# Large tiles at multiples of 128 bytes in each partition, in a kernel of attention beside a Fourier transform

## The chip, the cores and the metric

The kernel runs on one core of a Trainium2 chip. The metric is the time of one execution on the device, in microseconds, as a median of several runs. The engines of the core are called PE (TensorE; PEld is its loading of weights), DVE (VectorE), ACT (ScalarE), POOL (GpSimd) and SP (SyncE, which issues the DMAs here). SBUF is the memory on the chip, 128 partitions, in each of which a tile takes a run of bytes; "place" below is a tile's first byte in the partition.

## What is computed

Two independent results stand beside each other in the output: attention with 32 heads that share one key and one value head, and the real part of a two-dimensional Fourier transform by matrices.

```python
# A: x [1,2048,1024], wq [1024,1024], wk, wv [1024,32], wo [1024,1024]
q = (x @ wq) as 32 heads of 32;  k = x @ wk;  v = x @ wv
p = softmax(q k^T * 32**-0.5);   a = concat_heads(p v) @ wo
# B: x [1,2048,1024], dft_seq [2048,2048] and dft_hid [1024,1024], real and imaginary
y = dft_seq_re @ (x @ dft_hid_re^T) - dft_seq_im @ (x @ dft_hid_im^T)
return concatenate([a, y], axis=-1)        # float32
```

## The kernel before

All work is recorded into one fixed order by a planner (class `Plan`) that knows a time for each task and keeps a queue for each of ACT, DVE, POOL and SP; PE's order is chosen along with it (the loop over `n` at the end of `tile_kernel`). On the chip each engine works through its list in that order.

*Products.* The large products (queries, both transforms, the output projection) go by a scheme of seven products for eight blocks (`PRODUCTS`). Each operand is split into a high and a low part, and three matmuls of 128 x 128 x 512 make one product: low and high of the left, `ml` and `mh`, as weights, and low and high of the right, `rl` and `rh`, as the moving operand, summed in a PSUM bank `psb` (`product`). The raw loads come into `m` and `r`; results leave over `h` and `y`. In the first products the parts of x and of the small weights lie in the tiles `p`.

*Attention* runs in 32 units (a block of 512 queries by four heads), each with 32 row steps and 32 column steps. A row step (`row`) multiplies the moving `kst` (the keys) by weights from `qst` (the queries) into `pss`; DVE takes its largest value into `nm`, and ACT the exponentials, whose sums go to `ls`. A column step (`col`) multiplies the moving `qst` by weights from `kst` into `pst`, and ACT writes its exponentials into `p`. A burst (`pv`) multiplies several `p` by `v`. Between these, PE fills in the products. Towards the end the last projections take their weights partly from `p` and from `rb`.

*The turned tile.* At the end of a unit's row steps (`open_unit`, from `t1` on) the row maxima and sums become the constants that the queries need. `md`, 32 numbers in each partition, holds two exponentials while this is worked out (a subtraction on POOL, an Exp on ACT, a product on POOL, a sum on DVE). The result, `m2`, is turned by PE and copied by DVE into `mt` (48 x 128, function `mt`), and three DMAs take it from there: two into `qst`, one to DRAM (`U.rows` and `rd`, kept in `U.sent`).

*Places.* Tiles of the pools of the left side are laid one after the other from the low end, those of the right side from the high end downwards. `m2` has 3 x 16 x 4 = 192 bytes, so what follows it starts 64 bytes past a multiple of 128. The high end itself is 96 bytes past one, and all right tiles have 2048 bytes. As built:

| tiles | first byte, before | past a multiple of 128, before | the same, after |
|---|---|---|---|
| ident, kst, v, m2 | 16512, 17024, 25216, 27264 | 0 | 0 |
| p (6 x 8192 bytes), qst (3 x 8192) | 27456, 76608 | 64 | 0 |
| nm, ls, md, mt | 101184 to 101824 | 64 | 0 |
| h, y, rb, ov | 102368 to 120800 | 96 | 0 |
| mh, ml, rh, rl | 122848 to 206816 | 96 | 0 |
| raw m and r | 208864 to 227296 | 96 | 0 |

The parts of a tile that a matmul takes lie multiples of 512 bytes behind its start (in `p` and `qst`, of 2048 or 512), so an operand has its tile's remainder. The two wkv tiles of the first products alone have parts of 256 bytes.

Of the kernel before, what the change touches and what calls it, by code (L numbers as in the profile page):

```python
# [9 lines left out]
F32 = mybir.dt.float32  # L10
F32R = mybir.dt.float32r
AF = mybir.ActivationFunctionType
ALU = mybir.AluOpType
AX = mybir.AxisListType
# [3 lines left out]
P = 128  # L18
# [7 lines left out]
NC = 16  # L26
# [164 lines left out]
def tile_kernel(ctx: ExitStack, tc, xT, wq, wkv, wo, xbT, wT, cT, out):  # L191
    nc = tc.nc
    te = Ordered(tc, nc.tensor)
    act = Ordered(tc, nc.scalar)
    dve = Ordered(tc, nc.vector)
    gp = Ordered(tc, nc.gpsimd)
# [3 lines left out]
    plan = Plan()  # L200

    def pool(name, bufs, **kw):
        kw.setdefault("reuse_waits", "tile")
        return ctx.enter_context(tc.tile_pool(name=name, bufs=bufs, **kw))
# [16 lines left out]
    keep = pool("keep", 1)  # L221
# [3 lines left out]
    dve.memset(kst[96:P, :].bitcast(F32), 0.0)  # L225
    dve.memset(kst[96:98, :].bitcast(F32), 1.0)
    v = keep.tile([P, NC, DH], F32, name="v")
    m2 = keep.tile([P, 3, NC], F32, name="m2")

    ps_s = pool("ps_s", 2, space=PSUM)  # L230
    ps_t = pool("ps_t", 1, space=PSUM)
# [2 lines left out]
    NY, NHR, NP, NQS = 5, 3, 6, 3  # L234
    NRR, NRM = 17, 4
    NT = {"r": (3, 2), "m": (3, 2)}
    stage = {k: pool(f"stage_{k}", 1, side="right") for k in "rm"}
    ringp = {k: pool(f"ring_{k}", 1, side="right") for k in "rm"}
    shape = {"r": [P, W], "m": [P, 4, P]}
    raw = {k: [Ring(stage[k], f"{k}{a}", NT[k][a], shape[k], F32) for a in range(2)] for k in "rm"}  # L240
    ringn = {"r": NRR, "m": NRM}
# [11 lines left out]
    sm = pool("sm", 2)  # L253
# [368 lines left out]
    NU, SU, LEAD, PACE = len(units), 32, 12, 4  # L622
# [7 lines left out]
    def place_of(u, r):  # L630

        return (r % 16, r // 16) if u == 0 else divmod(r, 2)
# [115 lines left out]

    nmr = Ring(sm, "nm", 2, [P, 2, NC], F32)
    lsr = Ring(sm, "ls", 2, [P, 2, NC], F32)  # L750
    mdr = Ring(sm, "md", 1, [P, 2, NC], F32)
    rowT, colT = [Task() for _ in range(total)], [Task() for _ in range(total)]
    rexp, cexp = [Task() for _ in range(total)], [Task() for _ in range(total)]
    pvT = [[Task() for _ in bursts[u]] for u in range(NU)]
    pvC = [[Task() for _ in range(NC)] for _ in range(NU)]
    unit = []
# [6 lines left out]
    def open_unit(u):  # L763
        b, g = units[u]
        U = Unit()
# [4 lines left out]
        for r, (a, d) in enumerate((("qh", qh_d), ("ql", ql_d), ("qh", qh_d))):  # L770
            U.open.append(plan.task("sp", ISSUE, lambda r=r, d=d: move(
                U.q.tile[r * DH:(r + 1) * DH], d[b][g].rearrange("(h d) c -> d h c", d=DH)),
                deps=[landed[a, b, g]], order=U.open[:1], prio=at, kb=256))
        U.q.users += [rowT[u * SU + SU - 1], colT[u * SU + SU - 1]]
        U.nm, U.ls, U.md = nmr.take(), lsr.take(), mdr.take()
        mx = None
        for r in range(SU):
            s = u * SU + r
            i, j = place_of(u, r)

            def top(r=r, s=s, i=i, j=j):
# [3 lines left out]
            mx = plan.task("dve", 1.22, top, deps=[rowT[s], *(U.nm.deps if r == 0 else ())], prio=first_p + s - 44)  # L785
            plan.task("act", 1.22, lambda s=s, i=i, j=j: act.activation(
                rowps[s], rowps[s], AF.Exp, bias=U.nm.tile[:, j, i:i + 1], accum_out=U.ls.tile[:, j, i:i + 1]),
                deps=[mx], prio=first_p + s - 43.6, into=rexp[s],
                order=[cexp[s - SU - LEAD - EXTRA]] if s >= SU + LEAD + EXTRA else [])

        T = {}

        def dv(us, f, *deps):
            return plan.task("dve", us, f, deps=deps, prio=-1e4)

        def gv(us, f, *deps):
            return plan.task("pool", us, f, deps=deps, prio=-1e4, port=True)

        def least(to):
            dve.tensor_reduce(to, U.nm.tile.rearrange("p j i -> p i j"), axis=AX.X, op=ALU.min)  # L800

        def t1():
            mdr.make(U.md)
            least(m2[:, 2])
        prev = [unit[u - 1].turn.done] if u else []
        a = dv(0.2, t1, mx, *U.md.deps, *prev)
        c = dv(0.2, lambda: least(m2[:, 0].bitcast(F32R)), mx, *prev)
        a = gv(0.3, lambda: gp.tensor_sub(U.md.tile, m2[:, 2].unsqueeze(1).to_broadcast([P, 2, NC]), U.nm.tile), a)
        e = plan.task("act", 0.24, lambda: act.activation(U.md.tile, U.md.tile, AF.Exp), deps=[a], prio=-1e4)
        c = gv(0.3, lambda: gp.tensor_sub(m2[:, 1], m2[:, 2], m2[:, 0]), c, a)  # L810
        a = gv(0.3, lambda: gp.tensor_mul(U.md.tile, U.md.tile, U.ls.tile), e, rexp[u * SU + SU - 1], rexp[u * SU + SU - 2])
        a = dv(0.2, lambda: dve.tensor_reduce(m2[:, 2], U.md.tile.rearrange("p j i -> p i j"), axis=AX.X, op=ALU.add), a, c)
        U.nm.users.append(a)
        U.ls.users.append(a)
        U.md.users.append(a)
        a = dv(0.25, lambda: dve.reciprocal(m2[:, 2], m2[:, 2]), a)
        U.turn = Odd(lambda bank: te.transpose(bank[:3 * NC, :P], m2.rearrange("p a b -> p (a b)"), ident), [a, c], 0.2, -1)

        def mt():
            T["mt"] = sm.tile([3 * NC, P], F32, name="mt", bufs=1)  # L820
            dve.tensor_copy(T["mt"], U.turn.bank[:3 * NC, :P])
        a = U.turn.freed = dv(0.27, mt, U.turn.done, *(unit[u - 1].sent if u else []))
        odds.append(U.turn)
        U.rows = [plan.task("sp", ISSUE, lambda k=k: move(
            U.q.tile[96 + k:97 + k].rearrange("o h (t c) -> o (h t) c", c=P), T["mt"][k * NC:(k + 1) * NC]),
            deps=[a], prio=-1e4, kb=8) for k in range(2)]
        rd = plan.task("sp", ISSUE, lambda: sp.dma_start(r_d[u], T["mt"][2 * NC:]), deps=[a], prio=-1e3, kb=8)
        U.sent = [*U.rows, rd]
        U.rb = rbr.take()
        U.inv = []  # L830
        for h in range(4):
# [21 lines left out]
        for k in range(len(bursts[u])):  # L853
            def ad(k=k):
                if k == 0:
                    dve.tensor_copy(ovr.make(U.ov), pvps[u, k])
                else:
# [3 lines left out]
        a = plan.task(wide, {"dve": 0.77, "pool": 1.34}, lambda on: eng[on].tensor_mul(U.ov.tile, U.ov.tile, U.rb.tile),  # L861
                      deps=[U.add[-1], *U.inv], prio=-5, port=True)
# [41 lines left out]
    for u in range(NU):  # L904
        open_unit(u)
# [23 lines left out]
    T = 0.0  # L929
# [228 lines left out]
    while n < total:  # L1158
# [65 lines left out]
        T = max(T, min(ts))  # L1224
# [82 lines left out]
```

## Time and profile before

| | |
|---|---|
| median of 3 runs | 2727.79 us (2727.74 to 2730.84) |
| the profiled execution | 2728.83 us, of which the span of instructions 2727.1 us |
| PE busy | 2707.7 us, 13728 matmuls |
| ACT, DVE, POOL busy | 2202.4, 1984.2, 1614.9 us |
| PE's granted clock | full in every slice |

The profile is of one execution. A matmul's duration in it is modelled, since matmuls overlap, but its start is recorded; how fast PE really goes is read from the distance of starts. Idle time of an engine that does not hold up the others costs nothing.

### The profile page before, as it was taken

The numbers are of one execution on the slowest core, as the hardware profiler recorded it, in microseconds if no ns is written. First come the engines' busy times: TensorE is split into PE (matmuls) and PEld (weight loads), VectorE is DVE, ScalarE is ACT, GpSimd is POOL, SyncE is SP. The second block draws the span as 40 slices with busy tenths as digits, with TensorE's granted clock in tenths as the row PEclk, the third lists the DMA queues.
The fourth block names the chain that finished last, engine by engine and source line by source line (L and its number), as shares of the span: only waits on it lengthen the run. The fifth ranks groups of instructions, "written<-read, shape, count | busy, mean of one in ns | idle before, by whom it ended". The sixth has DMA issues, their size and how long they took to land.

```text
span 2727.1 us, 40980 instructions
## 1 busy us (share of the span) xinstructions
PE 2707.7 (99%) x13728; PEld 1913.3 (70%) x13728; DVE 1984.2 (73%) x2342; ACT 2202.4 (81%) x3209; POOL 1614.9 (59%) x1331
## 2 busy tenths in 40 slices
PE   8999999999999999999999999999999999999999
PEld 6876767676767676767767667676676766766666
DVE  7977686878777776676676676676677677668755
ACT  6688888787878788888888888888888888878743
POOL 3826574858674547556355255567867757455464
PEclk9999999999999999999999999999999999999999
DMA  9756586878886649548347355457858857344486
GB/s 291 243 174 223 198 263 193 280 242 286 269 276 195 220 155 287 165 151 267 101 144 259 97 160 158 144 174 244 285 181 265 288 150 243 113 138 136 141 270 209
DMA packets 348981, 564.16 MB, mean 207 GB/s; under 512 B 38496, under 2 KB 86880, under 8 KB 348768
## 3 DMA queue, kind: packets, MB, share of 16 engines
q1 hardware_dynamic: 348768, 561.53, 64.6%
q8 instruction: 108, 1.77, 0.3%
q14 instruction: 105, 0.86, 0.1%
HBM read 410.39 MB, written 149.95 MB: 205 GB/s over the span
## 4 chain that ended last, share of the span: by engine, by line
PE 93%; DMA 3%; POOL 1%; DVE 1%; ACT 1%; issue 1%; SPq 0%; DVEq 0%; POOLq 0%; ACTq 0%
PE psb L60 59%; PE pss L60 17%; PE pst L60 17%; DMA r<-a 0%; ACT pss L60 0%; DMA m<-in_cT_dram 0%; DMA qst<-in_xT_dram 0%; POOL rl L60 0%; DVE p L60 0%; ACT p L60 0%; DMA o<-ov 0%; DMA m<-in_wq_dram 0%; SPq L60 0%; DMA r<-in_xT_dram 0%; POOL ml L60 0%
## 5 line engine op out<-in xcount | busy, mean ns | idle before, releaser
L60 DVE TENSOR_REDUCE nm<-pss 128x1 f32<-128x1024 f32 x1024 | 1241.7, 1220 | 309.3 <-PE pss L60 303.2
L60 ACT ACTIVATE p<-pst 128x1024 f32<-128x1024 f32 x1024 | 1052.0, 1027 | 433.5 <-PE pst L60 432.9
L60 ACT ACTIVATE pss<-pss,nm 128x1024 f32<-128x1024 f32 x1024 | 1111.7, 1086 | 31.9 <-DVE nm L60 29.6
L60 POOL TENSOR_TENSOR ml<-m,mh 128x512 fp32r<-128x512 f32 (+1 forms) x382 | 494.8, 1296 | 496.0 <-DVE mh L60 329.4
L60 PE MATMUL psb<-rl,mh 128*128 128x512 f32 x1710 | 675.0, 395 | 1.5 <-POOL rl L60 1.5
L60 PE MATMUL psb<-rh,mh 128*128 128x512 f32 x1710 | 674.8, 395 | 1.4 <-DVE y L60 0.9
L60 PE MATMUL psb<-rh,ml 128*128 128x512 f32 x1710 | 674.3, 394 | 0.0
L60 PE MATMUL pss<-kst,qst 128*128 128x512 f32 x2048 | 652.0, 400 | 3.9 <-ACT pss L60 2.7
L60 PE MATMUL pst<-qst,kst 128*128 128x512 f32 x2048 | 639.0, 393 | 0.7 <-ACT p L60 0.4
L60 PEld LDWEIGHTS pss<-kst,qst 128*128 128x128 f32 x2048 | 375.3, 188 | 164.0 <-issue 71.2
L60 PE MATMUL psb<-p,v 128*32 128x512 f32 x4096 | 459.6, 595 | 0.0
L60 POOL TENSOR_TENSOR m<-m,m 128x512 f32<-128x512 f32 (+1 forms) x260 | 339.0, 1304 | 195.0 <-DMA m<-in_cT_dram 127.1
L60 PEld LDWEIGHTS pst<-qst,kst 128*128 128x128 f32 x2048 | 382.0, 188 | 100.0 <-ACT p L60 6.9
L60 PEld LDWEIGHTS psb<-rl,mh 128*128 128x128 f32 x1710 | 321.2, 188 | 76.6 <-POOL rl L60 3.0
L60 PEld LDWEIGHTS psb<-rh,mh 128*128 128x128 f32 x1710 | 321.3, 188 | 76.5 <-DVE y L60 1.3
L60 PEld LDWEIGHTS psb<-rh,ml 128*128 128x128 f32 x1710 | 321.2, 188 | 73.4
L60 PEld LDWEIGHTS psb<-p,v 128*32 128x32 f32 x4096 | 123.2, 110 | 283.3 <-issue 273.2
L60 POOL TENSOR_TENSOR rl<-r,rh 128x512 fp32r<-128x512 f32 x201 | 260.0, 1304 | 102.1 <-DVE rh L60 97.4
L60 POOL TENSOR_TENSOR y<-y,h 128x512 f32<-128x512 f32 x160 | 208.1, 1311 | 151.4 <-DVE h L60 141.2
L60 DVE TENSOR_REDUCE mh<-m 128x512 fp32r<-128x512 f32 x372 | 251.3, 676 | 25.2 <-PE psb L60 13.1
L60 POOL TENSOR_TENSOR r<-r,r 128x512 f32<-128x512 f32 x160 | 208.9, 1309 | 54.8 <-DMA r<-a 40.3
L60 ACT ACTIVATION_READ_ACCUMULATOR pss<-pss,nm 128x1 f32 x1024 | 208.5, 204 | 0.0
(94 smaller groups left out, 1002.8 us busy)
## 6 DMA issues: line engine op xcount, KB each, us to landing
m<-in_cT_dram SPq DMA_DIRECT2D x384, 256.0 KB, 3.9
r<-a SPq DMA_DIRECT2D x192, 256.0 KB, 4.5
y<-a SPq DMA_DIRECT2D x128, 256.0 KB, 3.9
a<-y SPq DMA_DIRECT2D x128, 256.0 KB, 3.0
r<-in_wT_dram SPq DMA_DIRECT2D x96, 256.0 KB, 3.9
m<-in_xbT_dram SPq DMA_DIRECT2D x96, 256.0 KB, 3.5
y<-y SPq DMA_DIRECT2D x96, 256.0 KB, 3.9
m<-in_wq_dram SPq DMA_DIRECT2D x80, 256.0 KB, 3.8
```

Of the source, the lines that this page charges most:

```text
L60: return lambda *a, **k: self.tc.keep_in_program_order(f(*a, **k))
```

## The change

`m2` gets a fourth row that nothing uses, so that it takes 256 bytes. A tile `pad` of 96 bytes is laid first on the right side. `md` is no longer a tile of its own: its 32 numbers take the first 128 bytes of the unit's `mt` tile, which `t1` now makes, and the turned result is copied over them. So the ring `mtr` of one buffer ties the first write of a unit to the DMAs of the unit before (`U.mt.users`), where before only the copy into `mt` waited for those. The last column of the table above is the outcome.

```diff
-    m2 = keep.tile([P, 3, NC], F32, name="m2")
+    m2 = keep.tile([P, 4, NC], F32, name="m2")[:, :3]
...
+    pool("pad", 1, side="right").tile([P, 24], F32, name="pad")
     stage = {k: pool(f"stage_{k}", 1, side="right") for k in "rm"}
...
-    mdr = Ring(sm, "md", 1, [P, 2, NC], F32)
+    mtr = Ring(sm, "mt", 1, [P, P], F32)
...
-        U.nm, U.ls, U.md = nmr.take(), lsr.take(), mdr.take()
+        U.nm, U.ls, U.mt = nmr.take(), lsr.take(), mtr.take()
...
         def t1():
-            mdr.make(U.md)
+            mtr.make(U.mt)
+            U.md = U.mt.tile[:, :2 * NC].rearrange("p (j i) -> p j i", j=2)
             least(m2[:, 2])
...
-        a = dv(0.2, t1, mx, *U.md.deps, *prev)
+        a = dv(0.2, t1, mx, *U.mt.deps, *prev)
...
-        U.md.users.append(a)
...
         def mt():
-            T["mt"] = sm.tile([3 * NC, P], F32, name="mt", bufs=1)
+            T["mt"] = U.mt.tile[:3 * NC]
             dve.tensor_copy(T["mt"], U.turn.bank[:3 * NC, :P])
-        a = U.turn.freed = dv(0.27, mt, U.turn.done, *(unit[u - 1].sent if u else []))
+        a = U.turn.freed = dv(0.27, mt, U.turn.done)
...
         U.sent = [*U.rows, rd]
+        U.mt.users += U.sent
```

On every engine the instructions stand in the same order as before; only the name `md` has become `mt`. What differs is which semaphores some of them wait for. On ACT, at the second unit's Exp (the row of `md` or `mt`, between a row step's exponentials `pss` and a column step's `p`), with what each waits for in brackets:

```order
 L60 ACTIVATE p<-pst 128x1024 [waits PE_49]
 L60 ACTIVATE pss,ls<-pss,nm 128x1024 [waits DVE_49,Activation_49]
-L60 ACTIVATE md<-md 128x32 [waits Pool_49]
+L60 ACTIVATE mt<-mt 128x32 [waits DMAHW1_49,DMAHW2_49,DMAHW0_49,Pool_49]
 L60 ACTIVATE p<-pst 128x1024 [waits PE_49]
 L60 ACTIVATE pss,ls<-pss,nm 128x1024 [waits DVE_49,Activation_49]
```

Nothing moved; the Exp now also waits for three DMA queues. This is so at 31 of its 32 places; two of POOL's subtractions into `mt` and two of the DMAs into `qst` name one semaphore more.

More of the change, by code (lines that the diff above doesn't have):

```diff
@@ L802, in t1 @@
         def t1():
-            mdr.make(U.md)
+            mtr.make(U.mt)
+            U.md = U.mt.tile[:, :2 * NC].rearrange("p (j i) -> p j i", j=2)
             least(m2[:, 2])
         prev = [unit[u - 1].turn.done] if u else []
-        a = dv(0.2, t1, mx, *U.md.deps, *prev)
+        a = dv(0.2, t1, mx, *U.mt.deps, *prev)
         c = dv(0.2, lambda: least(m2[:, 0].bitcast(F32R)), mx, *prev)
-        a = gv(0.3, lambda: gp.tensor_sub(U.md.tile, m2[:, 2].unsqueeze(1).to_broadcast([P, 2, NC]), U.nm.tile), a)
-        e = plan.task("act", 0.24, lambda: act.activation(U.md.tile, U.md.tile, AF.Exp), deps=[a], prio=-1e4)
+        a = gv(0.3, lambda: gp.tensor_sub(U.md, m2[:, 2].unsqueeze(1).to_broadcast([P, 2, NC]), U.nm.tile), a)
+        e = plan.task("act", 0.24, lambda: act.activation(U.md, U.md, AF.Exp), deps=[a], prio=-1e4)
         c = gv(0.3, lambda: gp.tensor_sub(m2[:, 1], m2[:, 2], m2[:, 0]), c, a)
-        a = gv(0.3, lambda: gp.tensor_mul(U.md.tile, U.md.tile, U.ls.tile), e, rexp[u * SU + SU - 1], rexp[u * SU + SU - 2])
-        a = dv(0.2, lambda: dve.tensor_reduce(m2[:, 2], U.md.tile.rearrange("p j i -> p i j"), axis=AX.X, op=ALU.add), a, c)
+        a = gv(0.3, lambda: gp.tensor_mul(U.md, U.md, U.ls.tile), e, rexp[u * SU + SU - 1], rexp[u * SU + SU - 2])
+        a = dv(0.2, lambda: dve.tensor_reduce(m2[:, 2], U.md.rearrange("p j i -> p i j"), axis=AX.X, op=ALU.add), a, c)
         U.nm.users.append(a)
         U.ls.users.append(a)
-        U.md.users.append(a)
         a = dv(0.25, lambda: dve.reciprocal(m2[:, 2], m2[:, 2]), a)
```

## Prediction

> **What bounds the kernel now.** I read the page's busy shares and its chain first, then what TensorE (PE) waits for in one long stage, then the distance from one matmul's start to the next.
>
> ```profile
> span 2727.1 us, 40980 instructions
> PE 2707.7 (99%) x13728; PEld 1913.3 (70%) x13728; DVE 1984.2 (73%) x2342; ACT 2202.4 (81%) x3209; POOL 1614.9 (59%) x1331
> PE 93%; DMA 3%; POOL 1%; DVE 1%; ACT 1%; issue 1%; SPq 0%; DVEq 0%; POOLq 0%; ACTq 0%
> ...
> 1100.00:2100.00 1000.00, 998.43 (x5125) 700.18 (x5124) 706.83 (x805) 853.16 (x1240) 582.59 (x482) 1.00 0.59 184
> ```
>
> PE is busy for 2707.7 of 2727.1 us, and in the thousand microseconds in the middle it idles 1.6 us, at a granted clock of 1.00, while ACT has 147 us to spare and the DMA engines are 59% busy. What remains on the other engines is cover. The time can move only if a matmul takes a different time to make way for the next one. The profiled execution took 2728.83 us, 1.0 us over the median of 2727.79; I sum against the former.
>
> The counts of the large matmuls (out<-moving,weights):
>
> ```profile
> L60 PE MATMUL psb<-rl,mh 128*128 128x512 f32 x1710 | 675.0, 395 | 1.5 <-POOL rl L60 1.5
> L60 PE MATMUL psb<-rh,mh 128*128 128x512 f32 x1710 | 674.8, 395 | 1.4 <-DVE y L60 0.9
> L60 PE MATMUL psb<-rh,ml 128*128 128x512 f32 x1710 | 674.3, 394 | 0.0
> L60 PE MATMUL pss<-kst,qst 128*128 128x512 f32 x2048 | 652.0, 400 | 3.9 <-ACT pss L60 2.7
> L60 PE MATMUL pst<-qst,kst 128*128 128x512 f32 x2048 | 639.0, 393 | 0.7 <-ACT p L60 0.4
> L60 PE MATMUL psb<-p,v 128*32 128x512 f32 x4096 | 459.6, 595 | 0.0
> ```
>
> The 395 ns are modelled ends; the real pace is between starts. So 3 x 1710 + 2 x 2048 = 9226 large matmuls set the time, and 0.2% of it, 5.5 us (about what a measurement of this kernel can tell from no change), is 0.6 ns on each of them.
>
> Pace in the body, from the chain of waits, at two starts of the same step, nine matmuls apart (two pst, four psb, two pss, one psb):
>
> ```profile
> 1103.27 0.46 PE pst L60 x2
> ...
> 1105.36 0.46 PE pst L60 x2
> 1105.81 0.93 PE psb L60 x4
> 1106.75 0.47 PE pss L60 x2
> ```
>
> 2.09 us over nine is 232.2 ns each. The timeline of PE near the end, where ACT and DVE have nearly nothing left, reads otherwise:
>
> ```profile
> 2702.98 0.39 PE L60 MATMUL pst<-rh,mh 128*128 128x512 f32 x1
> ...
> 2707.05 0.39 PE L60 MATMUL psb<-rh,mh 128*128 128x512 f32 x1
> ...
> 2711.14 0.39 PE L60 MATMUL pss<-rh,p 128*128 128x512 f32 x1
> ...
> 2715.35 0.39 PE L60 MATMUL psb<-rh,rb 128*128 128x512 f32 x1
> ...
> 2716.48 0.39 PE L60 MATMUL psb<-rh,rb 128*128 128x512 f32 x1
> 2712.74 1.29 DVE L60 COPY p<-pss 128x512 f32<-128x512 f32 x2 [6.53 <-PE pss L60]
> ```
>
> Eighteen matmuls lie between the first three starts each, eighteen to the fourth, five to the fifth. With moving r and weights m, both 96 bytes past a multiple of 128, they take 4.07/18 = 226.1 and 4.09/18 = 227.2 ns. With the same moving tiles and weights in p, which lies at 64, they take 4.21/18 = 233.9 ns. With weights in rb, at 96 again, 1.13/5 = 226.0. DVE sat idle for 6.5 us until 2712.74, so the slow stretch began before DVE had anything to do. The reverse mixture, moving p at 64 and weights m at 96, stands in the first products, and the pair kst (0) and qst (64) among them:
>
> ```profile
> 17.48 0.63 PE L60 MATMUL psb<-p,mh 128*128 128x512 f32 x2
> ...
> 23.78 0.63 PE L60 MATMUL psb<-p,mh 128*128 128x512 f32 x2
> ...
> 49.59 0.63 PE L60 MATMUL pss<-kst,qst 128*128 128x512 f32 x2
> 50.05 0.63 PE L60 MATMUL psb<-p,mh 128*128 128x512 f32 x2
> ```
>
> 27 matmuls in 6.30 us are 233.3 ns each; the pss pair, 0.46 us for two, 230. So a matmul whose two operands start alike in their 128 bytes makes way in about 226.4 ns, one whose operands start unlike in 230 to 234. That is what I take the change to act on.
>
> **The change, part by part.**
>
> *Addresses.* After it kst, qst, p, v, r, m, h, y, rb and ov all lie at 0 in their 128 bytes: every pair becomes alike. No row has a pair alike at 0, so the price is bounded. Below: if the body's whole excess over the quiet alike pace goes, 232.2 - 226.4 = 5.8 ns x 9226 = 53.5 us. Above: nothing goes, 0 (a loss is rival two). In between, by the nearest rows:
> - pss and pst, 4096 matmuls of kst and qst, unlike (0 and 64). Nearest is the pss pair at 230: 3.6 ns x 4096 = 14.7 us.
> - Some 240 products with an operand in p, at 233.6: 7.2 ns x 240 = 1.7 us.
> - The 5130 products of r and m are alike already, yet stand among the 232.2. The four psb of the step take 1106.75 - 1105.81 = 0.94 us, 235 each. Part of that is load that stays; part can be the weights of the unlike neighbour, since each step changes kind four times. No row separates them, so it is 0 to 8 ns; I take 1.5, near the lower end, because ACT and DVE are busy there and idle in the tail: 7.7 us.
>
> Together 24.1 us.
>
> *The bursts of p by v.* Their p moves from 64 to 0, v stays at 0.
>
> ```profile
> 1136.42 5.29 PE psb L60 x48
> L60 PEld LDWEIGHTS pst<-qst,kst 128*128 128x128 f32 x2048 | 382.0, 188 | 100.0 <-ACT p L60 6.9
> L60 PEld LDWEIGHTS pss<-kst,qst 128*128 128x128 f32 x2048 | 375.3, 188 | 164.0 <-issue 71.2
> L60 PEld LDWEIGHTS psb<-rh,mh 128*128 128x128 f32 x1710 | 321.3, 188 | 76.5 <-DVE y L60 1.3
> ```
>
> 48 records in 5.29 us are 441 ns for four at a time; loads of 32 columns leave little to meet. I take 0, between 0 and 3 ns in 441, 3 us in all. The three LDWEIGHTS rows, weights at 0, 64 and 96, all have 188 ns: an address by itself costs a load nothing, so if anything counts it is how two streams lie to each other.
>
> *The other engines' instructions.* Starting at 64 or at 96, ACT's copies agree:
>
> ```profile
> L60 ACT ACTIVATE mh<-m 128x512 fp32r<-128x512 f32 x15 | 9.2, 627 | 10.9 <-DMA m<-in_wq_dram 10.9
> L60 ACT ACTIVATE p<-qst 128x512 fp32r<-128x512 f32 x8 | 5.0, 631 | 1.8 <-DMA qst<-in_xT_dram 1.7
> ```
>
> 627 against 631 ns: 0, and under PE in any case. The same cover hides what transfers gain or lose.
>
> *The shared tile.* md moves into mt, so unit u's first write of it follows the three DMAs that read unit u-1's turned tile. ACT's Exp names these queues now, about 60 waiting instructions more.
>
> ```profile
> L60 ACT ACTIVATE md<-md x32: 218/228/244, 117.3 to 2577.5; 128x32 f32<-128x32 f32 x32
> ...
> L60 SPq DMA_DIRECT2D r<-mt x32: 330/569/1226, 126.6 to 2593.0; - x32
> ...
> DMA to landing us min/median/max: 1.6/1.9/4.9
> ```
>
> Units are (2577.5 - 117.3)/31 = 79 us apart; the last read is issued some 9 to 16 us after the Exp and lands at most 4.9 later, so the next Exp finds it done by over 55 us. What is left is the issue of the waits: 0 to 60 x 228 ns (the Exp itself, ACT's shortest) = 13.7 us of ACT, two at a time, under its 147 us of room in each thousand. Behind the Exp stand p<-pst and pss; PE fills such a delay of up to 0.46 us with products. I take 0; without that cover it would be up to 14 us.
>
> *Sum.* 2728.8 - 14.7 - 1.7 - 7.7 = 2704.7; against the median, 2704. ACT does not become the bound: PE would need 9 of ACT's 147 us in a thousand. The first 60 us, where PE waits for loads, and the last 10, which are DVE's, stay.
>
> **The rivals.**
>
> *One: no change, 2728.* The slow mixtures all have one operand in p or qst. These could be slow because of what happens beside them (DMA in the first 60 us, DVE from 2712.74 on), or because p lies far from r, which stays so. For it: the three equal LDWEIGHTS rows, and that 5130 alike products run at 232 in the body all the same. Against it: the 233.9 between two stretches at 226 to 227, within 9 us and with the same moving tiles. The Trainium skill's page SBUF — State Buffer, section "Who interferes with whom", speaks for this rival: it gives PE two independent read ports, one for the moving operand and one for LDWEIGHTS, and says that PE never waits on anyone. By that rule the 226 and the 234 could not differ by address, and the time would stay at 2728; the tail's rows do not sit well with it. The cachelines of 16 bytes in the same page's section "Specifications (TRN2)" would see no difference either; no run here shows such a line.
>
> *Two: slower, 2742.* One start for all could make streams meet that now miss each other: the moving read, the next weights, and the p that ACT writes would begin in the same place of their 128 bytes. The place is the pss and pst pairs, now unlike and at 230 to 232. For it: the alike psb products of the body have the worst pace there, 235. If all 9226 came to 235, that is +2.8 x 9226 = 25.8 us; half of them, +13, to 2742. It decides from 0.6 ns a matmul on. Against it: the alike pairs of the tail are the fastest of all.
>
> *Three: all of the excess goes, 2675.* The load's effect on the body's products would have to be one of unlike places too. For it: r and m at 96 run beside ACT writing p at 64. It is the lower end of my own case.
>
> **How the numbers follow.** Operands alike are faster, 2675 to 2722 with 2704 the likeliest: 0.62. No change, within 5.5 us: 0.26. Slower: 0.12, up to 2755. The range holds the first two, from 2675 to 2733, and leaves out the slower case and the tails of the first. Faster 0.62, same 0.26, slower 0.12.
>
> **What would show it.** In the profile after: the step of nine matmuls in the body at 2.06 us or less instead of 2.09; the eighteen products with weights in p at 4.08 us instead of 4.21, like their neighbours; the first 27 at 6.1 instead of 6.30. If those two quiet stretches become fast and the body does not, the mechanism is right and the size wrong. If they stay at 233, address had nothing to do with it, and rival one holds. If the stretch of r and m in the tail rises over 227, rival two does. ACT's waits would show as PE idle in the middle above 1.6 us per thousand.

## The result, and the profile after

The changed kernel takes 2689.2 us in the median of four runs (2687.53 to 2692.2), beside 2727.76 for the kernel before (2725.7 to 2730.84): a ratio of 0.9859, with a 95% interval of 0.9848 to 0.9871. That is 38.6 us less. The profiled execution took 2687.53 us, 41.3 us less than the one of before.

From the page: span, busy time of each engine, the chain's shares, and the groups of large matmuls (out<-moving,weights, count | busy us, modelled mean ns of one | idle time before).

```profile
span 2685.7 us, 41044 instructions
PE 2667.4 (99%) x13728; PEld 1911.9 (71%) x13728; DVE 1979.0 (74%) x2342; ACT 2168.1 (81%) x3209; POOL 1611.5 (60%) x1331
PE 91%; DMA 4%; DVE 2%; ACT 1%; POOL 1%; issue 1%; SPq 0%; DVEq 0%; POOLq 0%; ACTq 0%
...
L60 PE MATMUL psb<-rl,mh 128*128 128x512 f32 x1710 | 666.6, 390 | 1.6 <-POOL rl L60 1.6
...
L60 PE MATMUL pss<-kst,qst 128*128 128x512 f32 x2048 | 644.2, 396 | 2.2 <-DMA kst<-h 1.2
L60 PE MATMUL pst<-qst,kst 128*128 128x512 f32 x2048 | 635.1, 391 | 1.1 <-ACT p L60 0.7
...
L60 PE MATMUL psb<-p,v 128*32 128x512 f32 x4096 | 459.6, 594 | 0.0
```

PE is still the bound at 99%, and its busy time lost 40.3 us (2707.7 to 2667.4) of the 41.4 that the span lost. The groups of `rl,mh`, `pss` and `pst` are each shorter; the bursts `p,v` have not moved by 0.1 us.

The thousand microseconds in the middle (length, then busy us and instructions of PE, PEld, DVE, ACT, POOL, then clock, DMA share, GB/s):

```profile
1100.00:2100.00 1000.00, 999.06 (x5220) 711.84 (x5219) 713.06 (x815) 852.40 (x1260) 594.26 (x493) 1.00 0.60 190
```

5220 matmuls instead of 5125 in the same time, at the same clock, with 0.9 us of idling instead of 1.6. The 0.7 us less of waiting is nothing beside that; each matmul made way sooner. How much sooner is read from start to start, since the ends are modelled. In these thousand microseconds the mean distance from one large matmul to the next large one is 234.3 ns before (3436 distances) and 229.3 after (3489). Sorted by their place behind the last burst (or behind the last turning of `m2`), they are:

| distance behind the burst | before, ns (count) | after, ns (count) |
|---|---|---|
| the first | 334 (50) | 332 (52) |
| the second to the eleventh | 231.6 (447) | 230.5 (458) |
| all later ones | 233.0 (2939) | 227.3 (2979) |

Little but the last row moved. Of the later distances 98.6% are between 225 and 228 ns after the change, and 9% before.

The chain of waits in the body (start, us, what):

```profile
1087.60 0.45 PE pst L60 x2
1088.06 0.91 PE psb L60 x4
1088.96 0.45 PE pss L60 x2
1089.42 0.23 PE psb L60
1089.64 0.45 PE pst L60 x2
```

The step of nine takes 2.04 us, 226.7 ns each (2.09 before). Its four `psb`, whose operands were alike already, take 0.90 where they took 0.94.

The timeline of PE at the two quiet places of the prediction:

```profile
18.30 0.62 PE L60 MATMUL psb<-p,mh 128*128 128x512 f32 x2
...
24.46 0.61 PE L60 MATMUL psb<-p,mh 128*128 128x512 f32 x2
...
2665.79 0.39 PE L60 MATMUL psb<-rh,mh 128*128 128x512 f32 x1
...
2669.87 0.39 PE L60 MATMUL pss<-rh,p 128*128 128x512 f32 x1
...
2673.95 0.39 PE L60 MATMUL psb<-rh,rb 128*128 128x512 f32 x1
```

The 27 products from 18.30 on take 6.16 us (6.30 before). Near the end, eighteen products with weights `m` take 4.08 us and the eighteen with weights in `p` also 4.08, where they took 4.21.

Where the gain lies, by adding up the distance from every matmul's start to the next start, by kind, over the whole of both traces:

| matmuls | before, us | after, us | difference | prediction |
|---|---|---|---|---|
| `pss` | 490.6 | 482.2 | -8.4 | } -14.7 |
| `pst` | 480.1 | 475.4 | -4.7 | } |
| products of r and m | 1201.5 | 1174.6 | -26.9 | -7.7 |
| first products, moving `p` | 46.6 | 44.9 | -1.7 | -1.7 |
| bursts `p,v` | 452.8 | 452.8 | 0 | 0 |

The largest part comes from the pairs that the change did not make alike, since they were.

### The profile page after: what moved, and what is told of

Same layout as the page of the kernel before. It is cut to its first block, busy times and chain, and to the rows that moved or that the text cites. A ratio compares the mean times of both kernels' runs of the same rounds, so it can differ in the third digit from the quotient of the medians.

```text
span 2685.7 us, 41044 instructions
## 1 busy us (share of the span) xinstructions
PE 2667.4 (99%) x13728; PEld 1911.9 (71%) x13728; DVE 1979.0 (74%) x2342; ACT 2168.1 (81%) x3209; POOL 1611.5 (60%) x1331
## 4 chain that ended last, share of the span: by engine, by line
PE 91%; DMA 4%; DVE 2%; ACT 1%; POOL 1%; issue 1%; SPq 0%; DVEq 0%; POOLq 0%; ACTq 0%
PE psb L60 58%; PE pss L60 17%; PE pst L60 17%; DMA r<-a 1%; ACT pss L60 1%; DVE nm L60 1%; DMA m<-in_cT_dram 1%; DMA qst<-in_xT_dram 0%; ACT p L60 0%; POOL ml L60 0%; DMA ws<-r 0%; DVE p L60 0%; SPq L60 0%; DMA m<-in_wq_dram 0%; DMA r<-in_xT_dram 0%
## 5 line engine op out<-in xcount | busy, mean ns | idle before, releaser
L60 PE MATMUL psb<-rl,mh 128*128 128x512 f32 x1710 | 666.6, 390 | 1.6 <-POOL rl L60 1.6
L60 PE MATMUL psb<-rh,mh 128*128 128x512 f32 x1710 | 666.5, 390 | 1.5 <-DVE y L60 0.9
L60 PE MATMUL psb<-rh,ml 128*128 128x512 f32 x1710 | 666.0, 389 | 0.0
L60 PE MATMUL pss<-kst,qst 128*128 128x512 f32 x2048 | 644.2, 396 | 2.2 <-DMA kst<-h 1.2
```

Of the source, the lines that this page charges most:

```text
L60: return lambda *a, **k: self.tc.keep_in_program_order(f(*a, **k))
```

## The experiments

Three theories were open. *Own pair*: a matmul is slow where its own two operands are unlike. *Mixture*: an unlike matmul slows its neighbours too. *Load*: what ACT writes into `p` meets PE's reads by its place, and that went away with the change. Diffs are against the changed kernel; every ratio is to runs of the kernel before beside it on the same chip.

### The shared tile alone

```diff
-    m2 = keep.tile([P, 4, NC], F32, name="m2")[:, :3]
+    m2 = keep.tile([P, 3, NC], F32, name="m2")
-    pool("pad", 1, side="right").tile([P, 24], F32, name="pad")
```

> The kernel before with md kept inside mt and its waits, and every large tile where it was (kst and v at 0, p and qst at 64, the right side at 96). Alike theory (operands that start alike in their 128 bytes make way faster) and absolute theory (a start at a multiple of 128 is fast by itself): no change, 2728 us within 5. If the shared tile and its waits brought the gain: 2689.

2727.2 us, ratio 0.9998 (0.9989 to 1.0008). The middle again:

```profile
1100.00:2100.00 1000.00, 998.36 (x5127) 700.68 (x5126) 706.89 (x806) 853.89 (x1241) 583.42 (x484) 1.00 0.58 185
```

5127 matmuls and 1.6 us of idling, as before the change. The added waits cost nothing and sharing the tile brings nothing; the gain is all in the places.

### One side back

With `m2` of three rows again, `p`, `qst` and the small tiles lie at 64, the rest at 0:

```diff
-    m2 = keep.tile([P, 4, NC], F32, name="m2")[:, :3]
+    m2 = keep.tile([P, 3, NC], F32, name="m2")
```

> The changed kernel with m2 at 192 bytes again, so that p and qst (and the small nm, ls, mt) are back at 64; kst, v and the whole right side stay at 0. Alike theory: pss and pst are unlike again, and so are the products with p: at least 16 us come back (2705), up to all 39 (2728) if unlike neighbours slow the products of r and m. Absolute theory: only qst and p are off; the products of r and m stay at 226.7 ns, 2700 to 2708.

2726.88 us, 0.9990 (0.9981 to 0.9999): the gain is gone. With the pad left out instead, the right side lies at 96 and the left at 0:

```diff
-    pool("pad", 1, side="right").tile([P, 24], F32, name="pad")
```

> The changed kernel without pad: the right side (r, m, h, y, rb) back at 96, the left side at 0. Alike theory, own operands only: every pair but some 240 is still alike, 2691. Alike theory with neighbours: r and m are unlike kst and qst beside them, 2700 to 2728. Absolute theory: the 5130 products of r and m slow again at 232, pss and pst at 226.7: about 2715.

2729.39 us, 1.0004 (0.9994 to 1.0014): gone as well. The chain of waits of this kernel, over thirteen matmuls (two pst, three psb, two pss, three psb, two pss, one psb):

```profile
1088.47 0.47 PE pst L60 x2
...
1091.49 0.46 PE pst L60 x2
```

3.02 us over thirteen is 232.3 ns. Here `kst` and `qst` are alike, and so are r and m; all but some 240 large matmuls have operands that agree, and yet in the middle (1100 to 2100 us) the distances behind products of r and m have a mean of 233.6 ns, as slow as before (233.9; 227.7 with the change). In the tail, where products of r and m follow none but their own kind, they stay at 226 to 227 ns (`pst`). *Own pair* falls: what matters is that two kinds, each alike in itself at different places, follow each other.

### Everything at another common place

```diff
+    keep.tile([P, 16], F32, name="lead")
     ident = keep.tile([P, P], F32, name="ident")
...
-    pool("pad", 1, side="right").tile([P, 24], F32, name="pad")
+    pool("pad", 1, side="right").tile([P, 8], F32, name="pad")
```

> Every tile, kst and v included, starts 64 bytes past a multiple of 128 (a lead of 64 bytes on the left, a pad of 32 in place of 96 on the right). Alike theory: as the changed kernel, 2689. Absolute theory with multiples of 128: 2728 or more, since nothing lies at 0 any more. Absolute theory with multiples of 64: 2689 too.

2691.43 us, 0.9869 (0.9854 to 0.9884). All at 64 is as good as all at 0, so the multiple of 128 itself is worth nothing; the common place is.

### One tile unlike at a time

The pools of `p` and `qst` change places, with `m2` in a small pool between them, so that `p` alone lies at 64:

```diff
-    m2 = keep.tile([P, 4, NC], F32, name="m2")[:, :3]
...
-    pp = pool("pp", NP)
-    pr = Ring(pp, "p", NP, [P, 4, W], F32)
     qsp = pool("qsp", NQS)
     qr = Ring(qsp, "qst", NQS, [P, 4, W], F32R)
+    m2 = pool("mid", 1).tile([P, 3, NC], F32, name="m2")
+    pp = pool("pp", NP)
+    pr = Ring(pp, "p", NP, [P, 4, W], F32)
```

> The changed kernel with p alone at 64 (the pools of p and qst change places, m2 of 192 bytes between them; the small nm, ls, mt at 64 too). Everything that PE reads in the body outside the bursts stays at 0. If only PE's own operands count: 2690 to 2697, since p is read in the bursts and in 240 products. If ACT's writing of p disturbs PE unless it lies alike: 2715 to 2728.

2689.1 us, 0.9867 (0.9852 to 0.9882). `p` is what ACT writes all through the body, and PE reads it there only in the bursts. Its place has no part in the gain: *load* falls. With `qst` alone at 64 (`m2` between the pools in their old order):

```diff
-    m2 = keep.tile([P, 4, NC], F32, name="m2")[:, :3]
...
+    m2 = pool("mid", 1).tile([P, 3, NC], F32, name="m2")
     qsp = pool("qsp", NQS)
```

> The changed kernel with qst alone at 64 (m2 of 192 bytes between the pools of p and qst; the small nm, ls, mt at 64 too). If only PE's operands count: all that left_at_64 lost, 2722 to 2728, since pss and pst alternate with the products of r and m in every step. If ACT's writing of p was what cost time there: 2695 to 2705.

2724.88 us, 0.9990 (0.9980 to 1.0000). The chain of waits there:

```profile
1086.11 0.47 PE pst L60 x2
1086.58 0.70 PE psb L60 x3
1087.28 0.46 PE pss L60 x2
...
1089.11 0.47 PE pst L60 x2
```

Thirteen take 3.00 us, 230.8 ns, and the three alike products between the unlike `pst` and `pss` take 0.70, 233 each. One tile of the body out of step loses nearly all, on its neighbours too.

### How far apart, and in how many bytes

Both sides of the changed kernel happen to lie 128 bytes past a multiple of 256 (27456 + 64 = 27520 for `p`, 102368 - 96 = 102272 for `h`). With a pad of 32 bytes, the right side lies 64 past the left:

```diff
-    pool("pad", 1, side="right").tile([P, 24], F32, name="pad")
+    pool("pad", 1, side="right").tile([P, 8], F32, name="pad")
```

> The changed kernel with a pad of 32 bytes: the right side at 64, the left side at 0. If places have to agree in 128 bytes: as right_at_96, 2727 within 5. If agreeing in 64 bytes is enough: 2689. If the loss grows with the distance of the places (32 of 128 at right_at_96, 64 here): over 2732.

2714.86 us, 0.9959 (0.9945 to 0.9974), about a third of the gain. None of the three forecasts: agreeing in 64 bytes is not enough, and the loss does not grow with the distance. The chain of waits, over the same thirteen:

```profile
1086.04 0.46 PE pst L60 x2
...
1089.03 0.46 PE pst L60 x2
```

2.99 us, 230.0 ns. The next two put `m2` into the shared tile (`U.m2 = U.mt.tile[:, 2 * NC:5 * NC]`, three rows, in place of the tile of its own) and differ only in the pad, 224 or 96 bytes:

```diff
-    pool("pad", 1, side="right").tile([P, 24], F32, name="pad")
+    pool("pad", 1, side="right").tile([P, 56], F32, name="pad")
```

> Every large tile at a multiple of 128, but the right side (r, m, h, y, rb) 128 bytes from the left side within 256: a pad of 224 bytes; m2 lies in the shared mt tile to make room. If agreeing in 128 bytes is enough, as the change has it: 2689 within 5. If places have to agree in 256 bytes, as the pairs of places_alone say (0 with 128: 232.7 and 233.2 ns, 0 with 256: 227.1): the gain is lost although all tiles lie at multiples of 128, 2715 to 2728.

> The control of right_128_more: the same kernel, m2 in the shared tile too, with the pad of 96 bytes, so that both sides lie 128 bytes past a multiple of 256. Both theories: as the changed kernel, 2689 within 5. If putting m2 into the shared tile costs time by itself, more, and the comparison of the two stands for the place alone.

With 224, every large tile is at a multiple of 128, the right side at 0 and the left at 128 of 256: 2723.33 us, 0.9982 (0.9972 to 0.9991). With 96, both at 128 of 256: 2688.98 us, 0.9853 (0.9838 to 0.9867). The chain of waits of the former:

```profile
1087.98 0.46 PE pst L60 x2
...
1090.99 0.46 PE pst L60 x2
```

3.01 us over thirteen, 231.5 ns. This kernel does all that the change was said to do, multiples of 128 throughout, and has lost nearly all of the gain. The places must agree in 256 bytes.

### The pace by itself

Two small kernels leave the computation out and run series of 36 matmuls of 128 x 128 x 512 on constants; each was run once, at a granted clock of 1.00. In the code, which is shortened here, `x` is the moving operand, `w` the weights, and `PLACES` the bytes by which each is shifted (in the first a to g are 0, 16, 32, 64, 96, 128, 256; in the second a to i are 0, 32, 64, ... 256):

```diff
+    for a in PLACES:
+        for b in PLACES:
+            run([(a, b)])        # 36 times te.matmul(ps, w[b], x[a])
+    run([("a", "a"), ("d", "d")])    # in turn
+    run([("a", "d"), ("d", "a")])
```

> Leaves the computation out: matmuls on constants only, in series of 36 with one moving tile (xa, xb, xc, xd, xe, xf, xg) and one weights tile (wa to wg), whose data start 0, 16, 32, 64, 96, 128 and 256 bytes past the same multiple of 128; all 49 pairs, with the other engines idle. Then series that alternate two pairs, series beside ACT writing at 0, 32, 64, 96, beside DVE and POOL writing at 0 and 64, and one behind four fp32 bursts. Alike theory: 226.7 ns a matmul where the two places agree in 128 bytes (so with 128 and 256 too), 230 to 234 where they don't, whichever they are; beside ACT 226.7 as long as ACT's place agrees too. Independent read ports: 226.7 for all 49, and beside every engine. Absolute theory: 226.7 only with both at 0, 128 or 256.

From the first kernel's timeline: in turn alike at 0 and alike at 64, then crosswise; later series beside ACT and POOL, with one matmul `sy` between them.

```profile
416.43 0.39 PE L38 MATMUL psh<-xa,wa 128*128 128x512 f32 x1
...
424.76 0.39 PE L38 MATMUL psg<-xa,wd 128*128 128x512 f32 x1
...
433.15 0.40 PE L38 MATMUL psh<-xa,wa 128*128 128x512 f32 x1
...
466.86 8.32 PE L38 MATMUL psh<-xa,wa 128*128 128x512 f32 x36
467.23 7.37 ACT L38 ACTIVATE od<-src 128x1024 f32<-128x1024 f32 x7
...
475.02 0.39 PE L38 MATMUL sy<-xa,wa 128*128 128x512 f32 x1
...
534.62 8.56 PE L38 MATMUL psh<-xa,wd 128*128 128x512 f32 x36
543.02 0.39 PE L38 MATMUL sy<-xa,wa 128*128 128x512 f32 x1
...
568.66 8.32 PE L38 MATMUL psh<-xa,wa 128*128 128x512 f32 x36
569.83 6.76 POOL L38 TENSOR_TENSOR ua<-ua,oa 128x512 f32<-128x512 f32 x5
...
576.82 0.39 PE L38 MATMUL sy<-xa,wa 128*128 128x512 f32 x1
```

Alike at 0 alone goes at 226.7 ns; in turn with alike at 64 it goes at 8.33/36 = 231.4. Crosswise, where no matmul's own operands agree but each one's weights agree with the moving operand of the one ahead, it is 8.39/36 = 233.1. So neither the own pair nor the pair of neighbours is the whole rule. Beside ACT writing at 64 without a pause the alike series takes 8.16/36 = 226.7, and beside POOL too; an unlike one has 8.40/36 = 233.3 beside ACT. ACT's place (0, 32, 64 or 96) and DVE's writing (at 0 or 64) changed nothing either.

Two results of this kernel do not fit a rule of the difference alone. From the same timeline:

```profile
74.62 8.48 PE L38 MATMUL psg<-xb,wb 128*128 128x512 f32 x36
82.94 8.68 PE L38 MATMUL psh<-xb,wc 128*128 128x512 f32 x36
...
258.09 8.56 PE L38 MATMUL psg<-xe,wc 128*128 128x512 f32 x36
266.49 8.57 PE L38 MATMUL psh<-xe,wd 128*128 128x512 f32 x36
```

With both operands at 16 the series takes (82.94 - 74.62)/36 = 231.1 ns, though they are alike, and a moving operand at 16 is slow with all seven weights (230.0 to 236.8 over the last 23 distances of each series); weights at 16 beside a moving operand at 0, 32 or 256 go at 226.7. So being alike is enough only at the multiples of 32 that were tried. And moving at 96 with weights at 32 takes (266.49 - 258.09)/36 = 233.3, where the second kernel has 228.8 for the same two places behind another series. What ran before, or the tiles' addresses beyond the last 256 bytes, must make that difference; no run separates the two.

> Leaves the computation out: series of 36 matmuls on constants, moving tiles xa to xi and weights wa to wi whose data start 0, 32, 64, ... 224 and 256 bytes past one multiple of 128, all 81 pairs; then series that alternate the pair at 0 with the pair at 32, 128, 160, 224 or 256, and series in which each sixth or each twelfth matmul is of the pair at 128 (or 256). Agreement in 256: 226.7 ns on the diagonal and for 0 with 256, 228 to 237 for most others. Agreement in 128: also for 0 with 128, 32 with 160 and so on. Alternating two pairs that are alike in themselves: 230 or more if the places of neighbours count (226.7 with 256), 226.7 for all if only a matmul's own pair counts. One odd matmul in six: if it takes some five matmuls to settle, as in places_alone, the series of sixths are slow throughout and those of twelfths half; if only the odd one pays, 227.5 and 227.

From the second kernel's timeline:

```profile
42.75 8.53 PE L38 MATMUL psg<-xa,we 128*128 128x512 f32 x36
51.12 8.55 PE L38 MATMUL psh<-xa,wf 128*128 128x512 f32 x36
59.51 8.40 PE L38 MATMUL psg<-xa,wg 128*128 128x512 f32 x36
67.75 8.56 PE L38 MATMUL psh<-xa,wh 128*128 128x512 f32 x36
76.15 8.32 PE L38 MATMUL psg<-xa,wi 128*128 128x512 f32 x36
84.31 8.57 PE L38 MATMUL psh<-xb,wa 128*128 128x512 f32 x36
...
726.97 1.30 PE L38 MATMUL psg<-xa,wa 128*128 128x512 f32 x5
728.10 0.39 PE L38 MATMUL psg<-xe,we 128*128 128x512 f32 x1
...
735.27 1.31 PE L38 MATMUL psh<-xa,wa 128*128 128x512 f32 x5
736.42 0.39 PE L38 MATMUL psh<-xi,wi 128*128 128x512 f32 x1
...
743.45 2.66 PE L38 MATMUL psg<-xa,wa 128*128 128x512 f32 x11
...
751.74 2.71 PE L38 MATMUL psh<-xa,wa 128*128 128x512 f32 x11
```

Weights 128 bytes from the moving operand: (51.12 - 42.75)/36 = 232.5 ns. 256 bytes from it: (84.31 - 76.15)/36 = 226.7, as fast as none. In this kernel, with all places at multiples of 32, the mean distance of starts over the last 23 of each series depends on the difference of places alone, to 0.5 ns (80 of the 81 pairs; the first series begins at a lower clock and is left out):

| weights minus moving, bytes modulo 256 | 0 | 32 | 64 | 96 | 128 | 160 | 192 | 224 |
|---|---|---|---|---|---|---|---|---|
| ns | 226.7 | 233.4 | 233.4 | 234.1 | 232.7 | 233.2 | 228.8 | 233.3 |

The table gives the prediction's quiet rows of before: weights in `p` at 64 and moving r at 224 of 256 differ by 96 (233.9 there, 234.1 here), moving `p` and weights `m` by 160 (233.3 there, 233.2 here).

One matmul at 128 among five at 0, each alike in itself, makes all six slow: (735.27 - 726.97)/36 = 230.6, with four still fast ones ahead of the first odd one. One at 256 does not: (743.45 - 735.27)/36 = 227.2, with the settling from the series ahead. One at 128 among eleven slows nearly the whole series, (751.74 - 743.45)/36 = 230.3, where half of it was expected. Behind the last odd matmul of that series, ten distances read 234, 231, 233, 236, 224, 231, 236, 228, 232, 231, and then 226.7 returns; behind the last one of the series of sixths only three are slow (231, 233, 231). Of the 16 alike series at multiples of 32 that follow a slow, unlike one, over both kernels, ten are fast from their first distance on, and the others take one to nine. So an odd matmul's effect lasts, and for how long is not fixed. The body of the kernel changes its kind every one to four matmuls, and before the change only 9% of its later distances were between 225 and 228 ns.

## Why the prediction was right, and where its sizes were off

- *PE's pace is the only thing that can move, and unlike places slow it.* Right, and shown: the gain is in distances of starts, comes and goes with places alone (0.9853 to 1.0004 among kernels that do the same work), and the bare series show it without any other work. But the prediction took a matmul's own pair as what counts, and that is a part of it only: `right_at_96` has nearly all pairs alike and none of the gain, and the pairs that the change made alike gave 13.1 + 1.7 of the 41.3 us.
- *`pss` and `pst`, 14.7 us.* Measured 13.1.
- *The 240 products with an operand in `p`, 1.7 us.* Measured 1.7 on those of the first 60 us, which the table counts. About half of that is pace: the distances under 260 ns, 183 in both, add up to 42.7 and 41.8 us, and the rest is a few waits. The tail's stretch is at 4.08 us, as foretold.
- *The products of r and m, 7.7 us.* This is the term that was mis-sized: 26.9. The prediction left it at 0 to 8 ns and chose 1.5, near the lower end, because ACT and DVE are busy beside them. That reason was wrong. Load costs these matmuls nothing (226.7 beside ACT, DVE and POOL; `p_at_64` keeps the whole gain). What went is what the prediction named as the other possibility, the unlike neighbour: 1201.5 us to 1174.6 over 5130 is 5.2 ns each. With 26.9 in its place the sum is 24.1 - 7.7 + 26.9 = 43.3 us, against 41.3 seen.
- *Why not all 53.5 us of rival three.* The bound set all 9226 to 226.4; the mean in the middle after the change is 229.3. The later distances did come down to 227.3, but the first behind each burst (334 to 332) and the next ten (231.6 to 230.5), together a seventh of all, hardly moved. In the bare series, too, a burst is followed by one of 337 ns and four of 229 to 235. The time came out midway between rival three's 2675 and the 2704, but that rival's reason, ACT writing `p` at 64 beside r and m at 96, is refuted by `p_at_64`.
- *Bursts and shared tile, 0 each.* Measured 0 (452.8 us in both; 0.9998 for the shared tile alone). The bursts' weights lie by turns at 0 and 128 of 256, before and after, since the part of `v` that a matmul takes is 128 bytes (it is the exception to the multiples of 512 named above the prediction). PE idles 0.9 us in the middle, under the 1.6 named.
- *Rival one, no change.* Refuted. Its rows of equal loads read true: LDWEIGHTS still have 188 ns in the page. But it is the distance of starts that changes, and that row can't show it: in the second bare kernel the loads of a series at 226.7 ns (`xa,wi`) and of one at 232.5 (`xa,we`) have 188 ns alike. The Trainium skill's page SBUF — State Buffer, section "Who interferes with whom", which stood for this rival, is half borne out: ACT, DVE and POOL, each writing beside PE, cost it nothing here. The same section calls PE's two read ports independent; the 226.7 and 233.4 ns by the place of one operand against the other do not agree with that, though no run shows that it is at the ports where the two meet.
- *Rival two, a common start collides.* Refuted twice, by all at 0 and all at 64.
- *"Alike in their 128 bytes".* Right for this change by luck. The rows before could not tell 128 from 256, since no two operands of the large matmuls there lay 128 apart in 256; `right_128_more` would have been taken for the same change, and is 34 us slower than its twin `right_alike_256` (2723.3 beside 2689.0).

What stays open is why: what in the chip has a period of 256 bytes, why 192 costs 2 ns and 64 costs 6.7, why the pace remembers what ran before, why a moving operand at 16 is slow beside all weights, and why two kinds 128 apart in strict turn cost only 1.7 ns in the bare series (228.4) where the kernel with its sides 128 apart runs at 231.5.

## What to carry to other kernels

Where PE is the bound, look at the built addresses of every tile that it reads, moving and weights, and bring them all to one place modulo 256 bytes. Which place does not matter among the multiples of 32 that were tried; both at 16 was slow. One tile out of step lost nearly everything (`qst_at_64`), and agreement within each matmul alone is not enough. Tiles that PE does not read in that stretch may lie anywhere. Measure the pace from start to start over a dozen matmuls or more, since modelled durations and the loads' own rows hide it, and a single odd matmul was felt for three more in one series and for ten in another.

## What the runs showed of the hardware

The distance between large matmuls is 226.7 ns at best and 228.8 to 234.1 by the difference of the two operands' places modulo 256 bytes, at a granted clock of 1.00 and with places at multiples of 32; one pair (96 and 32) had 233.3 in one kernel and 228.8 in the other. With the moving operand at 16 it is 230.0 to 236.8. An odd matmul's effect lasted for three more in one series and ten in another. Writing by ACT, DVE or POOL beside PE, at any place tried, left 226.7 as it was.
